# A decode block whose scheduler context is closed behind the first loads

## The chip, the cores and the metric

The kernel runs on one core of a Trainium2 chip. The metric is the device time of one execution in microseconds (us). A time stands for the median of several executions; a profile is one further execution, recorded instruction by instruction, and its span runs from the first to the last recorded instruction.

## What is computed

The reference is one decode step of a block with four sequences (B = 4), one new token each, and D = 512 channels. All numbers are 32-bit floats.

```python
xn = _layernorm(x, axis=-1)
return x + _A_ref(xn, A_k_cache, A_v_cache, A_wq, A_wo) + _B_ref(xn, B_w1, B_w2, B_w3, B_w4)
```

`_A_ref` is attention over a cache: 32 heads of 128 channels, 4096 cached keys and values per sequence and head. With `q = xn @ wq`:

```python
scores = jnp.einsum("bhqd,bhkd->bhqk", q, k_cache) * (Dh ** -0.5)
p = _softmax(scores, axis=-1)
o = jnp.einsum("bhqk,bhkd->bhqd", p, v_cache)
```

and `o`, with its heads side by side, is multiplied by `wo`. `_B_ref` has a token mixing that shifts along the sequence; with one token every shifted part is zero, so `x1 = xn`, and what is left of it is `x1 + _gelu(_layernorm(x1) @ w3) @ w4`, with F = 1792 hidden channels. The two caches are 268 MB each and make up nearly all the data.

## The kernel before, in words

The caches are cut into 32 blocks of four heads (NJ = 32, LAST = 31). One block of K or of V is 128 partitions by 16,384 elements, 8 MB. There is room for three such blocks: `ks[0]` and `ks[1]`, which K uses in turn, and `vs`, which V uses. The weights borrow the same room: at the start w3 and several small tiles (`ident`, `wide`, `xs`, `lnc`) lie in `vs` and wq in `ks[1]`; at the end w4 comes into `vs`, the last V block into `ks[0]` and wo into `ks[1]`.

The order of the work is written out by hand. The whole program, but for its last wait, stands in one critical section (line 168) of a scheduling context: the scheduler doesn't reorder what is inside, and the kernel's own class `Steps` (lines 53 to 83) sets the semaphores. `do(engine, make, *after)` makes the engine wait for the listed steps, issues the instruction and lets it increment that engine's own semaphore (nPE, nDVE, nACT, nPOOL). `load` (line 165) does the same for a transfer, by default from SP's queue.

Setup (lines 175 to 264): SP issues the loads of w3, wq and K block 0 (k0), ACT the load of x. POOL makes `ident` and clears some tiles, DVE writes two constants, and then one chain runs: layer norm of x on DVE with its square root on ACT (L198 to L205), transpose on PE (L211), second layer norm, second transpose, the product with w3 (L234), GELU on DVE and ACT (L238 to L247), the query product with wq (L255), scaling and transposes of q (L259 to L262).

The loads of the caches (lines 271 to 284) all stand in SP's queue, each behind a wait: K block 1 waits for the query product (it takes wq's place), V block 0 for GELU and q, each later K block for `summed` (DVE has reduced the block that was there) and each later V block for `done` (the block before has been used and copied). At the end SP issues w4 and five pieces of wo.

Three loops run side by side, one on each engine. DVE (L300) multiplies a K block by q (L320) and sums over channels (L321) in two halves, then takes the maximum of the rows. ACT (L334) makes the exponentials (L339) and copies results out of PSUM. PE (L384) multiplies the exponentials by the V block (L373) and selects and sums (L378, L380). The last V block stands behind the loop.

The ending: products with w4 (L396) and wo (L410, and L152 by quarter columns into `total`), a copy to SBUF (L421), and four stores of 2 KB, two on SP's queue and two on ACT's (L423), each of which adds 16 to the semaphore `out`. Then the critical section ends; a second one (line 427) holds one wait of SP for `out` to be 64. Where the context is left, the framework adds what the profile puts on lines 168, 427 and 452: drains, by which each engine reports that it has finished its instructions, semaphores and branches between the sections, then a barrier of all five engines, a clear of the semaphores by POOL, and a second barrier.

Of the kernel before, what the change touches and what calls it, by code (L numbers as in the profile page):

```python
# [44 lines left out]
P = 128  # L45
# [7 lines left out]
class Steps:  # L53
# [33 lines left out]
def decode_block(ctx: ExitStack, tc: tile.TileContext, x, k, v, wq, wo, w3, w4, out):  # L87
# [61 lines left out]
    def blocks4(start, stop, w, m, src):  # L149
# [18 lines left out]
    with tc.tile_critical():  # L168
# [11 lines left out]

        ident0 = do("POOL", lambda e: e.memset(ident, 0.0))

        ident_ok = do("POOL", lambda e: e.affine_select(
            out=ident, in_=ident, compare_op=ALU.not_equal, fill=1.0, base=0, pattern=[[-1, P]],
            channel_multiplier=1), ident0)
        xnT = X.rearrange("p c b -> p (c b)").rearrange("p (c m) -> p c m", c=NC)
        x1nT = lts[:, 0].rearrange("p h q -> p (h q)").rearrange("p (c m) -> p c m", c=NC)
        xnT0 = do("POOL", lambda e: e.memset(xnT, 0.0))
        x1nT0 = do("POOL", lambda e: e.memset(x1nT, 0.0))
        rs0 = do("POOL", lambda e: e.memset(rs, 0.0))  # L190
        ones_ok = do("DVE", lambda e: e.memset(ones, 1.0))
        eps_ok = do("DVE", lambda e: e.memset(eps, EPS))


        lnq = os.rearrange("p m d -> p (m d)")[:B, :]

        def layernorm(src, o, s, *after):
            d = do("DVE", lambda e: e.reduce_sum(s[:, 0:1], src, axis=AX.X), *after)  # L198
            d = do("DVE", lambda e: e.tensor_scalar_mul(s[:, 0:1], s[:, 0:1], 1.0 / D), d)
            d = do("DVE", lambda e: e.tensor_scalar(lnc, src, s[:, 0:1], None, op0=ALU.subtract), d)  # L200
            d = do("DVE", lambda e: e.tensor_mul(lnq, lnc, lnc), d)
            d = do("DVE", lambda e: e.reduce_sum(s[:, 1:2], lnq, axis=AX.X), d)
            a = do("ACT", lambda e: e.activation(s[:, 2:3], s[:, 1:2], AF.Sqrt, bias=eps[:B], scale=1.0 / D), d, eps_ok)
            d = do("DVE", lambda e: e.reciprocal(s[:, 3:4], s[:, 2:3]), a)
            return do("DVE", lambda e: e.tensor_scalar_mul(o, lnc, s[:, 3:4]), d)  # L205

        def transposed(src, o, p, *after):

            do.wait("PE", after)
            for c in range(NC):  # L210
                i = lambda e: e.matmul(p[:, c, :], src.rearrange("b (p c) -> b c p", c=NC)[:, c, :], ident[:B, :B],  # L211
                                       start=True, stop=True)
                d = do("PE", i)
            return do("DVE", lambda e: e.tensor_copy(o[:, :, 0:B], p), d, xnT0, x1nT0)

        pw_row = pw.rearrange("p g m -> p (g m)")
        xn, x1n = pw_row[:B, 0:D], pw_row[:B, D:2 * D]
        ptn = pt.rearrange("p (n c b) -> p n c b", n=32, c=NC)
        xn_ok = layernorm(xs, xn, lns[:B, 0], x_in)
        sel_ok = do("DVE", lambda e: e.reduce_sum(sel, ident.rearrange("p (q m) -> p m q", q=G), axis=AX.X), ident_ok)  # L220
        mask_ok = do("DVE", lambda e: e.reduce_sum(mask, ident.rearrange("p (q m) -> p q m", q=G), axis=AX.X))
        xnT_ok = transposed(xn, xnT, ptn[:, 0], xn_ok, ident_ok)
        x1n_ok = layernorm(xn, x1n, lns[:B, 1], xn_ok)

        do.wait("PE", [x_in])
        blocks4(True, False, ident[:B, 0:32], 32, xs)
        total_ok = do("PE", lambda e: blocks4(False, False, ident[:B, 0:32], 32, xn))
        x1nT_ok = transposed(x1n, x1nT, ptn[:, 1], x1n_ok, xnT_ok)


        do.wait("PE", [x1nT_ok, w3_in])
        for c in range(NC):
            for t in range(4):
                up = lambda e: e.matmul(y[32 * t:32 * t + 32, :FT], x1nT[:, c, :], w3_sb[:, c, t * FT:(t + 1) * FT],  # L234
                                        start=(c == 0), stop=(c == NC - 1))
                d = do("PE", up)
        hs, u, th, gt = (vs[:, n * FT:(n + 1) * FT] for n in range(4))
        a = do("ACT", lambda e: e.copy(hs.rearrange("p (m i) -> p m i", i=32),  # L238
                                       y[:, :FT].rearrange("p (i m) -> p m i", i=32)), d)
        d = do("DVE", lambda e: e.tensor_mul(u, hs, hs), a)  # L240
        d = do("DVE", lambda e: e.tensor_scalar(u, u, GELU_B, 1.0, op0=ALU.mult, op1=ALU.add), d)
        d = do("DVE", lambda e: e.tensor_mul(u, u, hs), d)
        a = do("ACT", lambda e: e.activation(th, u, AF.Tanh, scale=GELU_A), d)
        d = do("DVE", lambda e: e.tensor_scalar(th, th, 1.0, 0.5, op0=ALU.add, op1=ALU.mult), a)
        d = do("DVE", lambda e: e.tensor_mul(hs, hs, th), d)
        d = do("DVE", lambda e: e.transpose(gt, hs), d)
        gT_ok = do("DVE", lambda e: e.tensor_copy(gT, gt.rearrange("p (m i) -> p m i", i=32)[:, :, 0:B]), d)  # L247


        wq_h = wq_sb.rearrange("p c (n j h d) -> p c n h j d", n=2, j=4, h=G)  # L250
        do.wait("PE", [xnT_ok, wq_in])
        for c in range(NC):
            for n in range(2):
                for h in range(G):
                    q = lambda e: e.matmul(pq[n][HP * h:HP * h + HP, :], xnT[:, c, :], wq_h[:, c, n, h],  # L255
                                           start=(c == 0), stop=(c == NC - 1))
                    pq_ok = do("PE", q)
        for n in range(2):
            a = do("ACT", lambda e: e.mul(pw_row[:, n * 4 * DH:(n + 1) * 4 * DH], pq[n], DH ** -0.5), pq_ok)  # L259
        d = do("DVE", lambda e: e.transpose(wide, pw_row), a)  # L260
        pw_ok = do("POOL", lambda e: e.memset(pw, 0.0), d)
        qT_ok = do("DVE", lambda e: e.tensor_copy(  # L262
            qT.rearrange("p (b i) n -> p b i n", b=B),
            wide.rearrange("p (i n m) -> p m i n", n=DH // HP, m=32)[:, 0:B]), d)
# [3 lines left out]
        SUMMED = [(sems["summed"], 2 * j + 2) for j in range(NJ)]  # L268
        DONE = [(sems["done"], j + 1) for j in range(NJ)]
        HALF = R * DH // 2  # L270
        load(ks[1], rows(kf, 1), "k1", None, pq_ok)
        load(vs, rows(vf, 0), "landed", None, gT_ok, qT_ok, total_ok)
        parts = [load(ks[0][:, n:n + HALF], rows(kf, 2)[:, n:n + HALF], f"half{i}", 16, (sems["summed"], i + 1))
                 for i, n in enumerate((0, HALF))]
        for j in range(LAST - 1):
            if j > 0:
                load(ks[j % 2], rows(kf, j + 2), f"k{j % 2}", None, SUMMED[j])
            load(vs, rows(vf, j + 1), "landed", None, DONE[j])
        last_in = load(ks[(LAST - 1) % 2], rows(vf, LAST), "last", 16, SUMMED[LAST - 1])
        w4_in = load(w4_sb, w4.rearrange("(p m) n -> p m n", m=NF), "w4", 16, DONE[LAST - 1])  # L280
        do.wait("SP", [SUMMED[LAST]])
        wo_r = wo.rearrange("(p c) n -> p c n", c=WC)
        for (c0, c1), sem in zip(wo_cuts, wo_sems):
            nc.sync.dma_start(wo_sb[:, c0:c1], wo_r[:, c0:c1]).then_inc(sem, 16)  # L284
        def take(engine, sem, n=1):

            engine.wait_ge(sems[sem], n)
            engine.sem_inc(sems[sem], -n)  # L288
# [11 lines left out]
        with nc.Fori(0, NJ // 2, engines=OrderedEngineSet([DVE]), head_slot={DVE: 128}) as j:  # L300
            e, n = nc.vector, 0

            def step(i, done="dve"):
                nonlocal n
                if n:
                    i.wait_op(sems["dve"], n, "sem-ge")
# [150 lines left out]
```

## Time and profile before

| | |
|---|---|
| time before, median of 3 runs | 1305.08 us (1304.96 to 1305.3) |
| span of the profiled execution | 1303.1 us |
| TensorE clock granted, mean over the span | 0.629 |
| DVE busy | 1164.2 us, 89% |
| PE busy | 366.4 us, 28% |
| ACT busy | 93.1 us, 7% |
| read from HBM | 561.00 MB |

The profiled execution has no separate time of its own beside its span. In the profile's rows, PE is TensorE, DVE is VectorE, ACT is ScalarE, POOL is GpSimd and SP is SyncE; a q behind the name (SPq) stands for the engine's sequencer, which issues transfers and handles semaphores and is not counted as busy. A row of the timeline gives the start, the length, the engine, the source line, the operation, what is written and read, and in brackets how long the engine was idle before and what ended that. A row by source line gives a count, the least, the median and the greatest duration in nanoseconds, and the start of the first and the last instruction. Tiles stand without their buffer number, so `ks` is either of `ks[0]` and `ks[1]`.

### The profile page before, as it was taken

How to read it: one execution, taken by the hardware profiler on the slowest of the kernel's cores; microseconds unless marked ns; L12 is line 12 of the kernel's file. 1: busy time of each engine (PE TensorE's matmuls, PEld its weight loads, DVE VectorE, ACT ScalarE, POOL GpSimd, SP SyncE). 2: the span in 40 equal slices, each digit the busy share in tenths (PEclk: the TensorE clock that was granted, in tenths of full speed). 3: DMA queues.
4: the chain of work that ended last, by engine and by line, in shares of the span. 5: the costliest groups of instructions: out<-in, count | busy, mean ns of one | idle time of the engine just before them, and what ended most of it. 6: DMA issues, size and time to landing. Idle time of an engine off the chain costs nothing. (4 is left out here: it accounts for less than half of the span.)

```text
span 1303.1 us, 6697 instructions
## 1 busy us (share of the span) xinstructions
PE 366.4 (28%) x2652; PEld 131.4 (10%) x2652; DVE 1164.2 (89%) x324; ACT 93.1 (7%) x330; POOL 2.4 (0%) x12
## 2 busy tenths in 40 slices
PE   3221233321233331133332123332122332113237
PEld 1000111100011110011110011110001111001112
DVE  3499999999999999999999999999999999999990
ACT  1000000000000000000000000000000000000000
POOL 0000000000000000000000000000000000000000
PEclk8655666655666665666665666665566666566668
DMA  9999999999999999999999999999999999999998
GB/s 403 444 422 445 428 439 430 435 430 437 430 428 441 424 445 424 445 424 441 428 439 430 437 430 435 433 428 439 424 445 424 445 424 443 426 439 430 437 422 350
DMA packets 10559, 561.10 MB, mean 431 GB/s; under 512 B 1188, under 2 KB 1204, under 8 KB 1464
## 3 DMA queue, kind: packets, MB, share of 16 engines
q1 hardware_dynamic: 10528, 561.00, 99.6%
q8 instruction: 4, 0.07, 0.0%
q14 instruction: 3, 0.02, 0.0%
q10 hardware_dynamic: 24, 0.01, 0.0%
HBM read 561.00 MB, written 0.01 MB: 431 GB/s over the span
## 5 line engine op out<-in xcount | busy, mean ns | idle before, releaser
L320 DVE TENSOR_TENSOR ks<-ks,qb 128x8192 f32<-128x8192 f32 x64 | 556.3, 8692 | 60.4 <-DVEq L288 55.4
L321 DVE TENSOR_REDUCE sc<-ks 128x64 f32<-128x8192 f32 x64 | 555.9, 8686 | 2.2
L373 PE MATMUL pv<-vs,pw 128*32 128x512 f32 x1984 | 284.3, 737 | 872.8 <-PEq L288 872.8
L373 PEld LDWEIGHTS pv<-vs,pw 128*32 128x32 f32 x1984 | 78.0, 132 | 1054.6 <-issue 1054.6
L344 ACT COPY os<-pv 128x512 f32<-128x512 f32 x32 | 18.8, 586 | 825.1 <-ACTq L288 825.1
L339 ACT ACTIVATE pw<-sc,small 32x128 f32<-32x128 f32 x128 | 51.0, 398 | 278.0 <-ACTq L288 276.8
L378 PE MATMUL poz<-sel,os 128*128 128x4 f32 x256 | 32.8, 252 | 28.2 <-PEq L288 28.2
L378 PEld LDWEIGHTS poz<-sel,os 128*128 128x128 f32 x256 | 31.0, 191 | 56.3 <-issue 56.3
L339 ACT ACTIVATION_READ_ACCUMULATOR pw<-sc,small 32x1 f32 x128 | 23.5, 184 | 0.0
L260 DVE STREAM_TRANSPOSE vs<-pw 128x1024 f32<-128x1024 f32 x1 | 1.2, 1245 | 17.2 <-ACT pw L259 17.2
L421 DVE COPY sc<-total 128x128 f32<-128x128 f32 x1 | 0.3, 290 | 16.4 <-PE total L152 16.4
L326 DVE TENSOR_REDUCE small<-sc 128x1 f32<-128x128 f32 x32 | 9.2, 286 | 4.7
L354 DVE RECIPROCAL rz<-oz 128x96 f32<-128x96 f32 (+1 forms) x2 | 1.1, 552 | 12.4 <-ACT oz L346 12.3
L380 PE MATMUL poz<-rs,ones 128*128 128x4 f32 x64 | 11.7, 253 | 0.0
L312 DVE STREAM_TRANSPOSE qb<-qg 128x128 f32<-128x128 f32 x32 | 10.0, 311 | 1.1
L311 DVE COPY qg<-qT 128x4 f32 x32 | 5.4, 170 | 5.5 <-issue 4.7
L380 PEld LDWEIGHTS poz<-rs,ones 128*128 128x128 f32 x64 | 9.7, 192 | 0.0
L346 ACT COPY oz<-poz 128x8 f32 x32 | 5.3, 166 | 50.9 <-ACTq L288 50.9
L410 PE MATMUL y<-ks,X 128*4 128x512 f32 x48 | 7.8, 818 | 3.5 <-DMA ks<-in_A_wo_dram 3.5
L255 PE MATMUL pv<-ks,X 128*32 128x512 f32 x32 | 5.0, 709 | 12.3 <-DMA ks<-in_A_wq_dram 12.3
L373 PE MATMUL pv<-ks,pw 128*32 128x512 f32 x64 | 8.3, 674 | 0.0
L327 DVE STREAM_TRANSPOSE tr<-small 128x32 f32<-128x32 f32 x32 | 6.8, 212 | 1.1
(72 smaller groups left out, 67.1 us busy)
## 6 DMA issues: line engine op xcount, KB each, us to landing
ks<-in_A_k_cache_dram SPq DMA_DIRECT2D x2, 4096.0 KB, 26.9
vs<-in_B_w_dram SPq DMA_DIRECT2D x2, 3584.0 KB, 13.6
ks<-in_A_wo_dram SPq DMA_DIRECT2D x1, 4096.0 KB, 21.7
ks<-in_A_wo_dram SPq DMA_DIRECT2D x1, 2048.0 KB, 26.3
ks<-in_A_wo_dram SPq DMA_DIRECT2D x1, 1024.0 KB, 28.3
ks<-in_A_wo_dram SPq DMA_DIRECT2D x1, 768.0 KB, 29.7
ks<-in_A_k_cache_dram SPq DMA_DIRECT2D x31, 42.2
vs<-in_A_v_cache_dram SPq DMA_DIRECT2D x31, 26.9
```

Of the source, the lines that this page charges most:

```text
L311: step(e.tensor_copy(qg, pairs[:, s, bass.ds(j, 1)].rearrange("p o n -> p (o n)")))
L312: step(e.transpose(qb.rearrange("p (n m) -> p n m", m=HP), qg.unsqueeze(2).to_broadcast([P, DH // HP, HP])))
L320: step(e.tensor_tensor(out=kt, in0=kt, in1=qb.unsqueeze(1).to_broadcast([P, w, DH]), op=ALU.mult))
L321: step(e.reduce_sum(sc[s][:, c:c + w], kt, axis=AX.X))
L326: step(e.reduce_max(rm, sc[s], axis=AX.X))
L327: step(e.transpose(tr[s], rm.to_broadcast([P, HP])))
L339: i = nc.scalar.activation(pw[hp, :, 4 * h:4 * h + 4], sc[s][hp, :].rearrange("p (g w) -> p g w", w=4), AF.Exp, bias=small[hp, s, 1:2], sc ...
L344: nc.scalar.copy(os, pv.rearrange("p (m d) -> p m d", m=4)).then_inc(sems["copied"], 1)
L373: i = nc.tensor.matmul(pv[32 * t:32 * t + 32, :], pw[:, g, :], vt[:, 4 * g:4 * g + 4, :], start=(g < 4), stop=(g >= NG - 4))
L378: nc.tensor.matmul(poz[:, 0:G], os[:, m, :], sel.rearrange("p (h m) -> p m h", m=4)[:, m, 0:G], start=(m == 0), stop=(m == 3))
L380: nc.tensor.matmul(poz[:, G:2 * G], ones.to_broadcast([P, P]), rs, start=True, stop=True).then_inc(sems["poz"], 1)
L410: i = nc.tensor.matmul(y[32 * t:32 * t + B, :], X[:, c, :], wo_sb[:, c], start=False, stop=(c >= 20))
```

## The change

Semaphores and tiles come straight from the core's program (`nc`) and not from the scheduling context (`tc`) and its pools. The critical section holds the first four loads alone; behind it the context is closed, which issues its drains, its two barriers and its semaphore clear at that place. All that follows has the same instructions in the same order, now one indentation further left and outside the context. At the end SP and ACT increment a new semaphore `bye` once their stores are issued; POOL waits for 2 and clears all the kernel's semaphores but `out`; SP waits for `out` and takes 64 off it.

```diff
-    def __init__(self, tc):
-        self.tc, nc = tc, tc.nc
+    def __init__(self, nc):
...
-        self.sem = {e: tc.alloc_semaphore(f"n{e}") for e in ("PE", "DVE", "ACT", "POOL")}
+        self.sem = {e: nc.alloc_semaphore(f"n{e}") for e in ("PE", "DVE", "ACT", "POOL")}
...
-    consts = ctx.enter_context(tc.tile_pool(name="consts", bufs=1))
-    psum = ctx.enter_context(tc.tile_pool(name="psum", bufs=1, space=PSUM))
-
     def sb(name, *shape):
-        return consts.tile([P, *shape], F32, name=name)
+        return nc.alloc_sbuf_tensor(name, [P, *shape], F32).ap()
 
     def bank(name):
-        return psum.tile([P, 4 * DH], F32, name=name)
+        return nc.alloc_psum_tensor(name, [P, 4 * DH], F32).ap()
...
-    do = Steps(tc)
-    sems = {n: tc.alloc_semaphore(n) for n in (
-        "x", "w3", "wq", "k0", "k1", "landed", "last", "w4", "go", "pv", "copied", "poz", "out",
-        "half0", "half1", "nm", "dve", "summed", "expd", "done")}
-    wo_sems = [tc.alloc_semaphore(f"wo{n}") for n in range(5)]
+    do = Steps(nc)
+    wo_sems = [nc.alloc_semaphore(f"wo{n}") for n in range(5)]
+    sems = {n: nc.alloc_semaphore(n) for n in (
+        "x", "w3", "wq", "k0", "k1", "landed", "last", "w4", "go", "pv", "copied", "poz",
+        "half0", "half1", "nm", "dve", "summed", "expd", "done", "bye", "out")}
...
         k_in = {0: load(ks[0], rows(kf, 0), "k0", 16)}
 
+    tc.close()
+    tc.compile()
+
...
-    with tc.tile_critical():
-        do.wait("SP", [stored])
+    nc.sync.sem_inc(sems["bye"], 1)
+    nc.scalar.sem_inc(sems["bye"], 1)
+    nc.gpsimd.wait_ge(sems["bye"], 2)
+    nc.clear_and_free_semaphores([*do.sem.values(), *wo_sems, *(h for n, h in sems.items() if n != "out")])
+    do.wait("SP", [stored])
+    nc.sync.sem_inc(sems["out"], -64)
```

More of the change, by code (lines that the diff above doesn't have):

```diff
@@ L178, in decode_block @@
         k_in = {0: load(ks[0], rows(kf, 0), "k0", 16)}
[L181 to L231, printed above, removed]
-        for c in range(NC):
[L233 to L257, printed above, removed]
@@ L258, in decode_block @@
-        for n in range(2):
[L259 to L288, printed above, removed]
@@ L383, in decode_block @@
-        do.wait("PE", [sel_ok, mask_ok, ones_ok, a])
-        with nc.Fori(0, LAST, engines=OrderedEngineSet([PE]), head_slot={PE: 0}):
-            values(lambda: take(nc.tensor, "landed", 16), vs)
-        xb = pt.rearrange("p (b c) -> p b c", b=B * 4)
-        for b in range(B - 1):
-            d = do("PE", lambda e: e.matmul(xb[:, b, :], lts[:, b].rearrange("p h q -> p (h q)"), sel, start=True, stop=True),
-                   LTS[b])
-        values(lambda: do.wait("PE", [last_in]), ks[(LAST - 1) % 2])
@@ L393, in decode_block @@
-        do.wait("PE", [w4_in, g4_ok])
-        for m in range(NF):
-            t, g, n = (m, g4[:, m, :], 32) if m < 4 else (m % 4, gT[:, m, :], B)
-            nc.tensor.matmul(y[32 * t:32 * t + n, :], g, w4_sb[:, m, :], start=(m < 4), stop=False)
-        d = do("PE", lambda e: e.matmul(xb[:, B - 1, :], lts[:, B - 1].rearrange("p h q -> p (h q)"), sel, start=True,
-                                        stop=True), LTS[B - 1])
-        X_ok = do("ACT", lambda e: e.copy(X.rearrange("p c b -> p b c"), xb[:, 0:B, :]), d)
@@ L420, in decode_block @@
-        r = sc[0]
-        d = do("DVE", lambda e: e.tensor_copy(r, total), d)
-        for t in range(4):
-            stored = do("SP" if t % 2 == 0 else "ACT", lambda e: e.dma_start(
-                out.rearrange("b s d -> (b s) d")[:, P * t:P * t + P], r[32 * t:32 * t + B, :]), d,
-                done=(sems["out"], 16, 64))
-    with tc.tile_critical():
-        do.wait("SP", [stored])
+    tc.close()
+    tc.compile()
+    ident0 = do("POOL", lambda e: e.memset(ident, 0.0))
+    ident_ok = do("POOL", lambda e: e.affine_select(
+        out=ident, in_=ident, compare_op=ALU.not_equal, fill=1.0, base=0, pattern=[[-1, P]],
+        channel_multiplier=1), ident0)
@@ new lines, in transposed @@
+    def transposed(src, o, p, *after):
+        do.wait("PE", after)
+        for c in range(NC):
+            i = lambda e: e.matmul(p[:, c, :], src.rearrange("b (p c) -> b c p", c=NC)[:, c, :], ident[:B, :B],
+                                   start=True, stop=True)
+            d = do("PE", i)
+        return do("DVE", lambda e: e.tensor_copy(o[:, :, 0:B], p), d, xnT0, x1nT0)
+    pw_row = pw.rearrange("p g m -> p (g m)")
+    xn, x1n = pw_row[:B, 0:D], pw_row[:B, D:2 * D]
+    ptn = pt.rearrange("p (n c b) -> p n c b", n=32, c=NC)
@@ new lines, in decode_block @@
+    xn_ok = layernorm(xs, xn, lns[:B, 0], x_in)
+    sel_ok = do("DVE", lambda e: e.reduce_sum(sel, ident.rearrange("p (q m) -> p m q", q=G), axis=AX.X), ident_ok)
+    mask_ok = do("DVE", lambda e: e.reduce_sum(mask, ident.rearrange("p (q m) -> p q m", q=G), axis=AX.X))
+    xnT_ok = transposed(xn, xnT, ptn[:, 0], xn_ok, ident_ok)
+    x1n_ok = layernorm(xn, x1n, lns[:B, 1], xn_ok)
+    do.wait("PE", [x_in])
+    blocks4(True, False, ident[:B, 0:32], 32, xs)
+    total_ok = do("PE", lambda e: blocks4(False, False, ident[:B, 0:32], 32, xn))
@@ new lines, in decode_block @@
+    x1nT_ok = transposed(x1n, x1nT, ptn[:, 1], x1n_ok, xnT_ok)
+    do.wait("PE", [x1nT_ok, w3_in])
+    for c in range(NC):
+        for t in range(4):
+            up = lambda e: e.matmul(y[32 * t:32 * t + 32, :FT], x1nT[:, c, :], w3_sb[:, c, t * FT:(t + 1) * FT],
+                                    start=(c == 0), stop=(c == NC - 1))
+            d = do("PE", up)
+    hs, u, th, gt = (vs[:, n * FT:(n + 1) * FT] for n in range(4))
+    a = do("ACT", lambda e: e.copy(hs.rearrange("p (m i) -> p m i", i=32),
+                                   y[:, :FT].rearrange("p (i m) -> p m i", i=32)), d)
@@ new lines, in decode_block @@
+    wq_h = wq_sb.rearrange("p c (n j h d) -> p c n h j d", n=2, j=4, h=G)
+    do.wait("PE", [xnT_ok, wq_in])
+    for c in range(NC):
+        for n in range(2):
+            for h in range(G):
+                q = lambda e: e.matmul(pq[n][HP * h:HP * h + HP, :], xnT[:, c, :], wq_h[:, c, n, h],
+                                       start=(c == 0), stop=(c == NC - 1))
+                pq_ok = do("PE", q)
+    for n in range(2):
+        a = do("ACT", lambda e: e.mul(pw_row[:, n * 4 * DH:(n + 1) * 4 * DH], pq[n], DH ** -0.5), pq_ok)
@@ new lines, in decode_block @@
+    d = do("DVE", lambda e: e.transpose(wide, pw_row), a)
+    pw_ok = do("POOL", lambda e: e.memset(pw, 0.0), d)
+    qT_ok = do("DVE", lambda e: e.tensor_copy(
+        qT.rearrange("p (b i) n -> p b i n", b=B),
+        wide.rearrange("p (i n m) -> p m i n", n=DH // HP, m=32)[:, 0:B]), d)
+    SUMMED = [(sems["summed"], 2 * j + 2) for j in range(NJ)]
+    DONE = [(sems["done"], j + 1) for j in range(NJ)]
+    HALF = R * DH // 2
+    load(ks[1], rows(kf, 1), "k1", None, pq_ok)
+    load(vs, rows(vf, 0), "landed", None, gT_ok, qT_ok, total_ok)
@@ new lines, in decode_block @@
+    parts = [load(ks[0][:, n:n + HALF], rows(kf, 2)[:, n:n + HALF], f"half{i}", 16, (sems["summed"], i + 1))
+             for i, n in enumerate((0, HALF))]
+    for j in range(LAST - 1):
+        if j > 0:
+            load(ks[j % 2], rows(kf, j + 2), f"k{j % 2}", None, SUMMED[j])
+        load(vs, rows(vf, j + 1), "landed", None, DONE[j])
+    last_in = load(ks[(LAST - 1) % 2], rows(vf, LAST), "last", 16, SUMMED[LAST - 1])
+    w4_in = load(w4_sb, w4.rearrange("(p m) n -> p m n", m=NF), "w4", 16, DONE[LAST - 1])
@@ new lines, in decode_block, with take @@
+    do.wait("SP", [SUMMED[LAST]])
+    wo_r = wo.rearrange("(p c) n -> p c n", c=WC)
+    for (c0, c1), sem in zip(wo_cuts, wo_sems):
+        nc.sync.dma_start(wo_sb[:, c0:c1], wo_r[:, c0:c1]).then_inc(sem, 16)
+    def take(engine, sem, n=1):
+        engine.wait_ge(sems[sem], n)
+        engine.sem_inc(sems[sem], -n)
+    nc.gpsimd.sem_inc(sems["expd"], 2)
+    do.wait("POOL", parts)
+    nc.gpsimd.sem_inc(sems["k0"], 16)
+    d = do("POOL", lambda e: e.memset(g4, 0.0), DONE[LAST - 1])
+    g4_ok = do("POOL", lambda e: e.tensor_copy(g4[:, :, 0:B], gT[:, 0:4, :]), d, gT_ok)
@@ new lines, in decode_block, with step @@
+    do.wait("DVE", [qT_ok])
+    pairs = qT.rearrange("p (j s) n -> p s j n", s=2)
+    with nc.Fori(0, NJ // 2, engines=OrderedEngineSet([DVE]), head_slot={DVE: 128}) as j:
+        e, n = nc.vector, 0
+        def step(i, done="dve"):
+            nonlocal n
+            if n:
+                i.wait_op(sems["dve"], n, "sem-ge")
+            i.then_inc(sems[done], 1)
+            n += done == "dve"
+        for s in range(2):
+            step(e.tensor_copy(qg, pairs[:, s, bass.ds(j, 1)].rearrange("p o n -> p (o n)")))
+            step(e.transpose(qb.rearrange("p (n m) -> p n m", m=HP), qg.unsqueeze(2).to_broadcast([P, DH // HP, HP])))
+            take(e, "expd")
+            take(e, f"k{s}", 16)
+            w = R // 2
+            for c in range(0, R, w):
+                kt = ks[s].rearrange("p (c d) -> p c d", c=R)[:, c:c + w]
+                step(e.tensor_tensor(out=kt, in0=kt, in1=qb.unsqueeze(1).to_broadcast([P, w, DH]), op=ALU.mult))
+                step(e.reduce_sum(sc[s][:, c:c + w], kt, axis=AX.X))
+                e.wait_ge(sems["dve"], n)
+                e.sem_inc(sems["summed"], 1)
+            rm, nm = small[:, s, 0:1], small[:, s, 1:2]
+            step(e.reduce_max(rm, sc[s], axis=AX.X))
+            step(e.transpose(tr[s], rm.to_broadcast([P, HP])))
+            step(e.tensor_reduce(nm, tr[s], axis=AX.X, op=ALU.max, negate=True), "nm")
+        take(e, "dve", n)
@@ new lines, in decode_block @@
+    do.wait("ACT", [pw_ok, rs0])
+    ozs = oz.rearrange("p n (j s h) -> p s n j h", s=2, h=G)
+    with nc.Fori(0, NJ // 2, engines=OrderedEngineSet([ACT]), head_slot={ACT: 128}) as j:
+        for s in range(2):
+            take(nc.scalar, "nm")
+            for h in range(G):
+                hp = slice(HP * h, HP * h + HP)
+                i = nc.scalar.activation(
+                    pw[hp, :, 4 * h:4 * h + 4], sc[s][hp, :].rearrange("p (g w) -> p g w", w=4), AF.Exp,
+                    bias=small[hp, s, 1:2], scale=1.0, accum_out=rs[hp, h:h + 1])
+            i.then_inc(sems["go"], 1)
+            take(nc.scalar, "pv")
+            nc.scalar.copy(os, pv.rearrange("p (m d) -> p m d", m=4)).then_inc(sems["copied"], 1)
+            take(nc.scalar, "poz")
+            nc.scalar.copy(ozs[:, s, :, bass.ds(j, 1)].rearrange("p n o h -> p n (o h)"),
+                           poz[:, 0:2 * G].rearrange("p (n h) -> p n h", n=2)).then_inc(sems["done"], 1)
@@ new lines, in decode_block, with spread @@
+    LTS = {}
+    def spread(b0, b1):
+        s = slice(H * b0, H * b1)
+        d = do("DVE", lambda e: e.reciprocal(rz[:, s], oz[:, 1, s]), DONE[ZB * b1 - 1])
+        d = do("DVE", lambda e: e.tensor_mul(ot[:, s], oz[:, 0, s], rz[:, s]), d)
+        n = H * (b1 - b0)
+        d = do("DVE", lambda e: e.tensor_mul(lts.rearrange("p b h q -> p (b h) q")[:, s],
+                                             ot[:, s].unsqueeze(2).to_broadcast([P, n, 4]),
+                                             mask.unsqueeze(1).to_broadcast([P, n, 4])), d)
+        LTS.update(dict.fromkeys(range(b0, b1), d))
@@ new lines, in decode_block, with values @@
+    spread(0, B - 1)
+    spread(B - 1, B)
+    def values(landed, rows_of):
+        take(nc.tensor, "go")
+        nc.tensor.sem_inc(sems["expd"], 1)
+        landed()
+        vt = rows_of.rearrange("p (c d) -> p c d", c=R)
+        for g in range(NG):
+            t = g % 4
+            i = nc.tensor.matmul(pv[32 * t:32 * t + 32, :], pw[:, g, :], vt[:, 4 * g:4 * g + 4, :],
+                                 start=(g < 4), stop=(g >= NG - 4))
+        i.then_inc(sems["pv"], 1)
+        take(nc.tensor, "copied")
+        for m in range(4):
+            nc.tensor.matmul(poz[:, 0:G], os[:, m, :], sel.rearrange("p (h m) -> p m h", m=4)[:, m, 0:G],
+                             start=(m == 0), stop=(m == 3))
+        nc.tensor.matmul(poz[:, G:2 * G], ones.to_broadcast([P, P]), rs, start=True,
+                         stop=True).then_inc(sems["poz"], 1)
@@ new lines, in decode_block @@
+    do.wait("PE", [sel_ok, mask_ok, ones_ok, a])
+    with nc.Fori(0, LAST, engines=OrderedEngineSet([PE]), head_slot={PE: 0}):
+        values(lambda: take(nc.tensor, "landed", 16), vs)
+    xb = pt.rearrange("p (b c) -> p b c", b=B * 4)
+    for b in range(B - 1):
+        d = do("PE", lambda e: e.matmul(xb[:, b, :], lts[:, b].rearrange("p h q -> p (h q)"), sel, start=True, stop=True),
+               LTS[b])
+    values(lambda: do.wait("PE", [last_in]), ks[(LAST - 1) % 2])
+    do.wait("PE", [w4_in, g4_ok])
@@ new lines, in decode_block @@
+    for m in range(NF):
+        t, g, n = (m, g4[:, m, :], 32) if m < 4 else (m % 4, gT[:, m, :], B)
+        nc.tensor.matmul(y[32 * t:32 * t + n, :], g, w4_sb[:, m, :], start=(m < 4), stop=False)
+    d = do("PE", lambda e: e.matmul(xb[:, B - 1, :], lts[:, B - 1].rearrange("p h q -> p (h q)"), sel, start=True,
+                                    stop=True), LTS[B - 1])
+    X_ok = do("ACT", lambda e: e.copy(X.rearrange("p c b -> p b c"), xb[:, 0:B, :]), d)
+    ys = os.rearrange("p m d -> p (m d)")
@@ new lines, in decode_block @@
+    do.wait("PE", [X_ok])
+    for (c0, c1), sem in zip(wo_cuts, wo_sems):
+        do.wait("PE", [(sem, 16)])
+        for c in range(c0, c1):
+            if c < 24:
+                t = (c + 2) % 4
+                i = nc.tensor.matmul(y[32 * t:32 * t + B, :], X[:, c, :], wo_sb[:, c], start=False, stop=(c >= 20))
+            else:
+                i = blocks4(False, c == WC - 1, X[:, c, :], B, wo_sb[:, c])
+        d = do("PE", lambda e: i)
+        if c1 == 24:
+            ys_ok = do("ACT", lambda e: e.copy(ys, y), d)
+        elif c1 == 28:
+            do.wait("PE", [ys_ok])
+            blocks4(False, False, sel, 32, ys)
@@ new lines, in decode_block @@
+    r = sc[0]
+    d = do("DVE", lambda e: e.tensor_copy(r, total), d)
+    for t in range(4):
+        stored = do("SP" if t % 2 == 0 else "ACT", lambda e: e.dma_start(
+            out.rearrange("b s d -> (b s) d")[:, P * t:P * t + P], r[32 * t:32 * t + B, :]), d,
+            done=(sems["out"], 16, 64))
+    nc.sync.sem_inc(sems["bye"], 1)
+    nc.scalar.sem_inc(sems["bye"], 1)
+    nc.gpsimd.wait_ge(sems["bye"], 2)
+    nc.clear_and_free_semaphores([*do.sem.values(), *wo_sems, *(h for n, h in sems.items() if n != "out")])
```

117 lines of the change are left out of this document (25 added, 92 removed).

## The prediction

> **What bounds the kernel now.** I read the page first: engine shares, queues, the slices.
>
> ```profile
> span 1303.1 us, 6697 instructions
> ...
> PE 366.4 (28%) x2652; PEld 131.4 (10%) x2652; DVE 1164.2 (89%) x324; ACT 93.1 (7%) x330; POOL 2.4 (0%) x12
> ...
> DMA  9999999999999999999999999999999999999998
> ...
> q1 hardware_dynamic: 10528, 561.00, 99.6%
> ```
>
> Queue q1 (SP's loads, 561 MB) keeps the 16 DMA engines busy for 99.6% of the span. DVE with 89% comes close but has room. The view by windows, cut at the four places where the stages change, shows where the other 0.4% lie (length of the stretch, busy time of the engines, then PEclk, DMA share, GB/s):
>
> ```profile
> 0.00:1.00 1.00, 0.00 (x0) 0.00 (x0) 0.00 (x0) 0.00 (x0) 0.26 (x5) 1.00 0.00 0
> ...
> 2.40:45.00 42.60, 18.49 (x128) 7.79 (x128) 13.27 (x29) 4.47 (x8) 0.95 (x1) 0.88 0.98 424
> 45.00:1298.50 1253.50, 346.86 (x2492) 122.89 (x2492) 1150.52 (x293) 87.71 (x322) 0.40 (x2) 0.62 1.00 433
> 1298.50:1303.10 4.60, 1.06 (x32) 0.67 (x32) 0.29 (x1) 0.00 (x0) 0.00 (x0) 0.80 0.02 5
> ```
>
> So time can be won or lost at three places only: the first microsecond, in which nothing is loaded; the last 4.6 us, in which nothing is loaded any more; and any moment between at which the queue would run dry. The chain that ended last says what those 4.6 us are (start, length, what):
>
> ```profile
> 1268.85 29.66 DMA ks<-in_A_wo_dram
> 1298.52 0.04 issue
> 1298.56 1.10 PE total L152 x32
> 1299.66 0.02 issue
> 1299.68 0.29 DVE sc L421
> ```
>
> The last piece of wo lands at 1298.5, PE and DVE finish at 1299.97. The remaining 3.2 us are stores and closing, which the chain leaves out; the view by source line has them (count, ns, start of the first and the last):
>
> ```profile
> L423 SPq DMA_DIRECT2D out_dram<-sc x2: 280/316/352, 1300.0 to 1300.4; - x2
> L423 ACTq DMA_DIRECT2D out_dram<-sc x2: 278/292/307, 1300.0 to 1300.3; - x2
> ...
> L168 SPq EVENT_SEMAPHORE  x3: 17/28/28, 1301.1 to 1301.4; - x3
> ...
> L168 SPq DRAIN  x1: 18/18/18, 1301.2 to 1301.2; - x1
> L168 SPq NOP  x1: 18/18/18, 1301.4 to 1301.4; - x1
> ...
> L452 SPq EVENT_SEMAPHORE  x1: 98/98/98, 1301.7 to 1301.7; - x1
> L452 SPq COMPARE_BRANCH  x1: 38/38/38, 1301.9 to 1301.9; - x1
> ...
> L427 SPq NOP  x1: 13/13/13, 1302.2 to 1302.2; - x1
> ...
> L452 SPq DRAIN  x2: 7/7/7, 1302.2 to 1302.3; - x2
> ...
> L452 POOLq DRAIN  x1: 106/106/106, 1302.5 to 1302.5; - x1
> ...
> L452 POOLq EVENT_SEMAPHORE_RANGE_CLEAR  x1: 225/225/225, 1302.6 to 1302.6; - x1
> ...
> L452 POOLq EVENT_SEMAPHORE  x1: 17/17/17, 1303.0 to 1303.0; - x1
> L452 SPq EVENT_SEMAPHORE  x1: 17/17/17, 1303.1 to 1303.1; - x1
> L452 PEldq EVENT_SEMAPHORE  x1: 51/51/51, 1303.1 to 1303.1; - x1
> ```
>
> The stores are issued from 1300.0 to 1300.7 (1300.4 + 0.3). The EVENT_SEMAPHORE of 98 ns at 1301.7 stands last before the branch; it is SP's wait for all four stores, and it ends at 1301.8. From there to the end, 1303.1 − 1301.8 = 1.3 us, only bookkeeping runs: a branch, SP's own drain and NOP, two barriers of all engines, and between them POOL's range clear of 225 ns.
>
> **The change, part by part.** *The end.* In the changed order of instructions SP issues its stores, adds one to bye, waits for out, and is done with that; nothing follows on any engine. What follows the wait in the rows above (1.3 us) is removed. The only new work is POOL's: wait for bye, drain, one range clear. SP's first instruction behind its stores stands at 1301.1 in the rows, so bye is complete by then at the latest; its drain and clear took from 1302.5 to 1302.8 in the old closing (1302.6 + 0.225), 0.3 us and at most 0.4; POOL is done by 1301.5, 0.3 us ahead of the end of the store wait. It sits beside the stores' flight and costs nothing. If that cover were gone (bye later than 1301.4), each later 0.1 us would cost 0.1 us. The gain at the end is 1.3 us; at least 0.9 (the two barriers alone, 1302.2 to 1303.1), at most 1.3 inside the span.
>
> That the wait ends at 1301.8 rests on the trace: the last store's issue starts at 1300.4, so issue to landing is 1.4 us. The Trainium skill, DMA: Bandwidth & Descriptors, section "Anatomy of one DMA — SWDGE (gpsimd) path", gives about 2.0 us fixed for one transfer, on another issuing path. By it the stores would land at 1302.4, an estimate from that page, and 0.7 us would be left to win (1304.4 us). The measured 1.4 us decides.
>
> *The beginning.* The closing block moves behind the four loads. Its rows:
>
> ```profile
> 0.94 0.20 POOL L181 MEMSET vs<- 128x128 f32 x1 [0.50 <-SPq L168]
> ...
> 1.02 0.06 DVE L191 MEMSET ones<- 128x1 f32 x1 [1.02 <-SPq L168]
> ...
> 1.38 0.29 POOL L183 TENSOR_SCALAR_AFFINE_SELECT vs<-vs 128x128 f32<-128x128 f32 x1 [0.23 <-POOL vs L181]
> ...
> 1.52 1.28 ACT L203 ACT_TABLE_LOAD   x1 [1.52 <-SPq L168]
> ...
> 1.89 0.42 SPq L166 DMA_DIRECT2D ks<-in_A_k_cache_dram  x1
> ...
> 2.51 0.67 DVE L198 TENSOR_REDUCE lns<-vs 4x1 f32<-4x512 f32 x1 [1.41 <-DMA vs<-in_A_x_dram]
> ...
> 5.33 0.29 ACT L203 ACTIVATE lns<-lns,eps 4x1 f32<-4x1 f32 x1 [2.53 <-DVE lns L202]
> ...
> 6.37 2.02 PE L211 MATMUL pt<-vs,pw 4*128 4x4 f32 x8 [6.37 <-DVE pw L205]
> ...
> 14.66 4.79 PE L234 MATMUL y<-vs,lts 128*32 128x448 f32 x32 [0.27 <-DVE lts L214]
> ...
> 31.72 1.08 PE L255 MATMUL pv<-ks,X 128*32 128x512 f32 x4 [12.27 <-DMA ks<-in_A_wq_dram]
> ...
> 40.52 0.33 SPq L166 DMA_DIRECT2D ks<-in_A_k_cache_dram  x1
> ...
> 51.99 8.69 DVE L320 TENSOR_TENSOR ks<-ks,qb 128x8192 f32<-128x8192 f32 x1 [6.72 <-DVEq L288]
> ```
>
> Nothing stands ahead of the first load that wasn't there, so the transfers begin as before. SP issues its third load until 1.89 + 0.42 = 2.31 and only then reaches the barriers. Priced by the old end, where the same kind of instructions ran: issue end to the NOP of L168, 1300.7 to 1301.4, 0.7; a branch, 0.2 (1301.9 to the next block); two barriers with the clear, 0.9. That opens the second barrier at 2.3 + 1.8 = 4.1 us. Least is 3.2 (barriers alone); most is 4.7 (the whole stretch from 1300.7 to 1303.1, store wait included, 2.4). DVE's two memsets (0.1 us) then precede L198, which starts at 4.2 instead of 2.51: 1.7 late, 0.8 to 2.3 between the bounds. ACT's table load then ends at 4.1 + 1.28 = 5.4, ahead of the square root that needs it (5.33 + 1.7 = 7.0). POOL starts 3.2 late, so ident is there at 1.67 + 3.2 = 4.9, ahead of the first transpose on PE, which waits for the norm anyway (6.37 + 1.7 = 8.1).
>
> Queued behind the delay is one chain: two norms, two transposes, the w3 product on PE, then the query product. PE stands idle 12.27 us before that product because wq hasn't landed. So 1.7 us late turns into 10.5 us of idle time in place of 12.27, the query product still starts at 31.72, and SP's next load (ks, 40.52) leaves on time. Cost zero, covered by the flight of wq. Without that cover it would be 1.7 us on k1's issue, and even that the queue absorbs: k0 is in flight until 52.0 (DVE's L320 waits for it), 11.5 us behind the issue at 40.52.
>
> *All else.* Tiles from pools become plain allocations, at the same places in SBUF and PSUM; loops, waits and every compute instruction stay. Cost zero; a bound can't be read from any row, since nothing changes that a row measures.
>
> **Sum.** The profiled execution: span 1303.1 us − 1.3 + 0 = 1301.8. The median of the runs is 1305.08, 1.98 above that span; kept, that gives 1305.08 − 1.3 = 1303.8 us, or 0.10% less.
>
> **The rivals.** *(1) The end gains more than its own 1.3 us.* PE and DVE are free at 1300.0 instead of 1303.1. If part of the 1.98 us outside the span is each engine's own closing, that part now overlaps the stores. For: the rows show all engines held in the two barriers until 1303.1. Against: SP, which the time then hangs on, still has its own share. With all of it saved 1301.8, with half 1302.8; as a rival with two thirds, 1302.5.
> The Trainium skill, Runtime: NRT & Kernel Launch, section "The launch sequence", speaks against this one: a barrier of all engines and a semaphore reset follow the kernel, so early engines would only wait there. No row here shows that stretch.
>
> *(2) No gain, 1305.1.* The engines have to meet somewhere; without the barriers the 1.3 us come back outside the span. For: 1.98 us outside are unexplained. Against: those two microseconds already stand behind barriers that met twice, and a fixed closing doesn't grow.
>
> *(3) Slower: the drain behind the loads waits for their data.* SP's DRAIN now stands behind three large loads (w3, wq, k0). If it held until k0 landed, the barrier would open at 52.0 + 0.9 = 52.9. From L198 to the end of the w3 product it takes 14.66 + 4.79 − 2.51 = 16.9 us, the query product 40.52 − 31.72 = 8.8: k1 would be issued at 78.6, and the DMA engines would stand idle for 26.6 us from 52.0. 1305.08 + 26.6 − 1.3 = 1330.4. It decides only from a point on: the delay must pass 12.3 (PE's idle time) + 11.5 (queue left) = 23.8 us before any DMA time is lost. Against: at the old end the SP DRAIN of L168 stood behind two stores, ran at 1301.2 for 18 ns, and the wait for those stores ended at 1301.8 only. A drain that waits for transfers would have ended there.
>
> *(4) The change doesn't do what it says.* The closing block could be emitted again at the end. The changed order of instructions has no barrier there; I put this with (2).
>
> **How the numbers follow.** Forecast 1303.8: 74%; its own range 1303.3 to 1304.5: on one side a quarter of what lies outside (0.5) on top, on the other the least gain of 0.9 (1304.2) and the 0.3 by which the three runs differ. Rival (1) 13%, as it needs a saving that no row shows; (2) with (4) 9%; (3) 4%, as one row contradicts it. The range 1302.2 to 1305.4 holds the forecast, (2) and most of (1), and leaves (3) out. A measurement of this kernel tells about 0.2% (2.6 us) from no change, so faster means under 1302.5: the lower part of (1), 11% in all; slower, over 1307.7: (3) and 1% unnamed, 5%; the same: 84%.
>
> **What would show it.** Right: a span near 1301.8; the last instruction SP's wait for out, ending 1.8 us behind the issue of the first store; POOL's range clear before it; two barriers and a clear between 2.3 and 5 us; L198's counterpart near 4.2; PE's idle time before the query product near 10.5; k1 issued near 40.5; q1 still at 99.6% or above. Wrong: a layer norm that starts behind 26 us, a DMA slice below 9 near the beginning, POOL's clear as the last instruction, or a span shorter by 1.3 with an unchanged time.

## The result and the profile after

The changed kernel takes 1303.33 us (median of 21 runs, 1303.17 to 1303.51) against 1305.08 us before (21 runs, 1304.89 to 1305.36): 1.75 us less, a ratio of 0.9986 with a 95% interval of 0.998 to 0.9992. The two ranges of the runs don't touch. The forecast was 1303.8 us, 1.3 less.

Each run, the profiled one too, has both a time and a span. Over the runs (21 of the changed kernel, 27 of the one before), the mean span went from 1303.29 to 1301.96 us (1.3 less, the forecast of the sum), and what lies outside it, time minus span, from 1.80 to 1.37 us. These further 0.43 us were in the prediction as a rival only. The page of the profile after:

```profile
span 1301.9 us, 6687 instructions
...
PE 367.0 (28%) x2652; PEld 132.2 (10%) x2652; DVE 1164.2 (89%) x324; ACT 93.0 (7%) x330; POOL 2.4 (0%) x12
...
q1 hardware_dynamic: 10528, 561.00, 99.7%
```

The loads still bound the kernel, with the same bytes. The end, by source line, in the changed kernel:

```profile
L422 SPq DMA_DIRECT2D out_dram<-sc x2: 273/310/347, 1300.1 to 1300.5; - x2
L422 ACTq DMA_DIRECT2D out_dram<-sc x2: 277/294/310, 1300.1 to 1300.4; - x2
...
L427 ACTq EVENT_SEMAPHORE  x1: 17/17/17, 1300.7 to 1300.7; - x1
...
L426 SPq EVENT_SEMAPHORE  x1: 17/17/17, 1300.8 to 1300.8; - x1
...
L429 POOLq DRAIN  x1: 99/99/99, 1300.8 to 1300.8; - x1
L429 POOLq EVENT_SEMAPHORE_RANGE_CLEAR  x1: 196/196/196, 1300.9 to 1300.9; - x1
...
L431 SPq EVENT_SEMAPHORE  x1: 17/17/17, 1301.9 to 1301.9; - x1
```

The issue of the last store begins at 1300.5 and SP's wait for all four ends the span at 1301.9, 1.4 us later, as before the change; the branch, the two barriers and the clear that stood behind it are gone. POOL is done at 1301.1, inside the stores' flight. The beginning, first by source line, then from the timeline:

```profile
L164 SPq DRAIN  x1: 55/55/55, 2.4 to 2.4; - x1
...
L177 SPq DRAIN  x3: 7/7/7, 2.7 to 3.0; - x3
...
L177 POOLq EVENT_SEMAPHORE_RANGE_CLEAR  x1: 51/51/51, 3.0 to 3.0; - x1
...
L177 SPq EVENT_SEMAPHORE  x2: 17/17/17, 2.9 to 3.3; - x2
```

```profile
3.48 0.67 DVE L197 TENSOR_REDUCE lns<-vs 4x1 f32<-4x512 f32 x1
...
31.84 1.94 PE L254 MATMUL pv<-ks,X 128*32 128x512 f32 x8 [11.55 <-DMA ks<-in_A_wq_dram]
...
40.93 0.33 SPq L162 DMA_DIRECT2D ks<-in_A_k_cache_dram  x1
...
52.03 8.69 DVE L319 TENSOR_TENSOR ks<-ks,qb 128x8192 f32<-128x8192 f32 x1 [6.33 <-DVEq L287]
```

SP's drain behind the loads takes 55 ns at 2.4 us, with all three large loads in flight, and the second barrier opens at 3.3. The first norm starts at 3.48 instead of 2.51, PE is idle 11.55 us before the query product instead of 12.27, and the first multiplication with K starts at 52.03 instead of 51.99. Most of the delay ended in the wait for wq, as forecast; K block 1 is issued 0.4 us later than before (40.93 against 40.52), which the start of that multiplication doesn't show.

### The profile page after: what moved, and what is told of

The parts are those of the page before. It is cut to its first block, busy times and chain, and to the rows that moved or that the text cites. A ratio compares the mean times of both kernels' runs of the same rounds, so it can differ in the third digit from the quotient of the medians.

```text
span 1301.9 us, 6687 instructions
## 1 busy us (share of the span) xinstructions
PE 367.0 (28%) x2652; PEld 132.2 (10%) x2652; DVE 1164.2 (89%) x324; ACT 93.0 (7%) x330; POOL 2.4 (0%) x12
```

## The experiments

All are the changed kernel with one edit. Where engines are held below, a new semaphore `end` makes them wait for SP at the very end (`take` waits for a semaphore and takes off what it waited for); POOL's clear leaves `end` out. The kernel before was measured beside each of them, with medians of 1305.00 to 1305.09 us; so times of kernels that weren't measured side by side compare to about 0.1 us only.

**1. Where the 0.43 us outside the span come from.** First, all four other engines are held until SP has waited for the stores:

```diff
     do.wait("SP", [stored])
     nc.sync.sem_inc(sems["out"], -64)
+    nc.sync.sem_inc(sems["end"], 4)
+    take(nc.tensor, "end")
+    take(nc.vector, "end")
+    take(nc.scalar, "end")
+    take(nc.gpsimd, "end")
```

> PE, DVE, ACT and POOL are held at the end until SP has waited for the stores; the closing block of before is not brought back. The span should end 0.1 us later than that of the changed kernel (1302.0 against 1301.9: one increment by SP, one wait and one decrement on each engine). Theory A (the 0.5 us that the change won outside the span come from engines that are done early): they are lost again, 1303.3 + 0.1 + 0.5 = 1303.9 us, and time minus span goes back from 1.4 to 1.9. Theory B (they come from the missing closing block itself, whenever the engines are done): 1303.4 us, time minus span stays at 1.4.

Measured: 1304.02 us (11 runs), mean span 1302.20, time minus span 1.89. The loss is back although the old closing block is not; theory A holds and B falls. Then POOL's drain and clear were moved behind the store wait:

```diff
-    nc.sync.sem_inc(sems["bye"], 1)
     nc.scalar.sem_inc(sems["bye"], 1)
-    nc.gpsimd.wait_ge(sems["bye"], 2)
-    nc.clear_and_free_semaphores([...])
     do.wait("SP", [stored])
     nc.sync.sem_inc(sems["out"], -64)
+    nc.sync.sem_inc(sems["bye"], 1)
+    nc.gpsimd.wait_ge(sems["bye"], 2)
+    nc.clear_and_free_semaphores([...])
```

> POOL's drain and range clear are put behind SP's wait for the stores, the cover of the stores' flight is taken away from them. Both theories: the span grows by what stands uncovered, drain 0.1 + clear 0.2 + two semaphore steps 0.1 = 0.4 us, to 1302.3. Theory A: POOL is late as well now, so the time grows by 0.4 us and by up to a further 0.5 if it is POOL's own closing that counts: 1303.7 to 1304.2 us. Theory B: 1303.7 us. If the clear had been free for another reason than its cover: 1303.3.

Measured: 1304.31 us (11 runs), 0.98 more. In the profiled execution the clear is the last thing in the span of 1302.4 us; by source line:

```profile
L428 SPq EVENT_SEMAPHORE  x1: 17/17/17, 1302.0 to 1302.0; - x1
...
L431 POOLq DRAIN  x1: 99/99/99, 1302.1 to 1302.1; - x1
L431 POOLq EVENT_SEMAPHORE_RANGE_CLEAR  x1: 196/196/196, 1302.2 to 1302.2; - x1
```

The span grew by 0.47 (mean 1302.43), the price of the uncovered clear; the other half, time minus span of 1.86 instead of 1.37, comes with POOL being last. So theory A was sharpened. Theory P: outside the span each engine has a closing of its own length, and the time is the latest of (engine's end + its closing). Its rival Q: the engines have to meet, so any engine held to the end costs the same. POOL alone, then PE alone was held, with the edit of the first run cut to one engine and an increment of 1:

> Only POOL is held until SP has waited for the stores; its range clear stays early. Theory P (each engine has a closing of its own outside the span, and POOL's is the longest): span 1302.0 to 1302.1, time minus span 1.9, so 1303.9 to 1304.0 us, as with all four engines held. Theory C (it was the late range clear, or another engine): 1303.4 to 1303.5 us, time minus span 1.4.

> Only PE is held. Theory P: PE's closing isn't longer than SP's, span 1302.1, time minus span 1.4, 1303.5 us. Theory Q (any engine that ends last beside SP costs the 0.5, because the engines have to meet): 1304.0 us.

POOL alone: 1303.99 us (11 runs), as much as all four together, with its clear as early as ever. By source line, the last instructions of that kernel and of the one that holds PE:

```profile
L431 SPq EVENT_SEMAPHORE  x1: 17/17/17, 1301.9 to 1301.9; - x1
...
L287 POOLq EVENT_SEMAPHORE  x1: 17/17/17, 1302.0 to 1302.0; - x1
```

```profile
L287 PEldq EVENT_SEMAPHORE  x1: 51/51/51, 1302.0 to 1302.0; - x1
```

In both the last instruction stands at 1302.0, yet the one with PE last takes 1303.73 us (11 runs), 0.26 less. Q falls: it matters which engine is last. P's guess that PE's closing is no longer than SP's was a miss; it lies between. Two more runs let another engine than SP wait for the stores:

```diff
-    do.wait("SP", [stored])
-    nc.sync.sem_inc(sems["out"], -64)
+    do.wait("DVE", [stored])
+    nc.vector.sem_inc(sems["out"], -64)
```

> DVE waits for the stores and takes 64 off out, SP ends at its bye (1300.8). Theory P: the time is the latest of the engines' ends plus each one's own closing; SP now ends early, POOL at 1301.1 + 1.9 = 1303.0, DVE at 1301.9 plus a closing that no run has shown. 1303.0 us if that is 1.1 or less, 1303.3 if it is as long as SP's 1.4. Theory Q: the engines meet, so 1303.3 us whoever waits.

> The same with ACT as the one that waits. Theory P: between 1303.0 us (ACT's closing 1.1 or less) and 1303.8 (1.9, as long as POOL's). Theory Q: 1303.3 us.

Measured: 1303.52 us with DVE, 1303.46 us with ACT (same edit with ACT), 11 runs each. Neither gains on SP. All runs by the engine that ends last (times are medians, spans and differences means over the runs):

| kernel | ends last | time | span | time − span |
|---|---|---|---|---|
| changed | SP | 1303.33 | 1301.96 | 1.37 |
| DVE waits for the stores | DVE | 1303.52 | 1302.09 | 1.47 |
| ACT waits for the stores | ACT | 1303.46 | 1301.96 | 1.51 |
| PE held | PE | 1303.73 | 1302.05 | 1.67 |
| before | all, at the barrier | 1305.09 | 1303.29 | 1.80 |
| POOL's clear last | POOL | 1304.31 | 1302.43 | 1.86 |
| all four held | four | 1304.02 | 1302.20 | 1.89 |
| POOL held | POOL | 1303.99 | 1302.09 | 1.90 |

(Before: 27 runs, beside those with all four held and with the clear last.) The five kernels further below, which also end with SP, have 1.36 to 1.40 in the last column. The kernel before fits as well: there POOL's last instruction stands 0.1 us ahead of the last one of all, and 1.90 − 0.1 = 1.80. What the engines do in that time no record shows, nor whether they meet there on ways of different length; that the time from the last instruction to the end depends on the engine, and that POOL's is the longest, is what the runs show.

**2. Whether the loads' flight is the cover at the beginning.** The context is closed ahead of the loads:

```diff
-    with tc.tile_critical():
+    tc.close()
+    tc.compile()
...
     k_in = {0: load(ks[0], rows(kf, 0), "k0", 16)}
-    tc.close()
-    tc.compile()
```

> The context is closed ahead of the four loads instead of behind them, so the two barriers and the clear stand in front of the first transfer. In the changed kernel they took 2.67 to 3.31 us, 0.64 us. If the loads' flight is what covers them there, the first load is issued at about 1.5 instead of 0.96 and the whole stream of loads shifts: 1303.3 + 0.55 = 1303.9 us. If the first microsecond didn't matter (the queue catches up later), 1303.3 us.

Measured: 1303.85 us (11 runs), 0.52 more. The timeline of SP in that kernel, and its last instruction by source line:

```profile
1.39 0.40 SPq L162 DMA_DIRECT2D vs<-in_B_w_dram  x1
```

```profile
L429 SPq EVENT_SEMAPHORE  x1: 17/17/17, 1302.4 to 1302.4; - x1
```

The first load leaves at 1.39 instead of 0.96, and the end comes 0.5 us later. The barriers that cost nothing behind the loads cost 0.5 us ahead of them. That is a little less than the 0.64 us that they take; the edit also removes the critical section, whose entry stood ahead of the loads.

**3. How much delay the setup can take.** The first norm was made to wait for a load as well, for w3, wq or k0:

```diff
+    do.wait("DVE", [w3_in])
     xn_ok = layernorm(xs, xn, lns[:B, 0], x_in)
```

> The first layer norm also waits for w3, so the setup's chain starts at 14.4 us instead of 3.5, 11 late, just within PE's 11.6 us of idle time ahead of the query product. Cover theory: the w3 product ends at 31.5, the query product starts where it did (31.8), 1303.3 us. If late microseconds counted: up to 1314.

> The first layer norm also waits for wq, so the chain of the setup starts at 31.8 us instead of 3.5, 28.3 late. In the changed kernel it takes 17.1 us from the norm to the end of the w3 product, so the query product starts at 48.9 instead of 31.8 and k1 is issued at 58.0 instead of 40.9. Cover theory: k0 has landed at 52.0, the queue is dry for 6 us and up to 2 more until the first bytes of k1: 1309.3 to 1311.3 us. If every late microsecond counted: 1303.3 + 28.3 = 1331.6. If the stream made up for it later: 1303.3.

> The first layer norm waits for k0, the price of the rival in which the drain behind the loads holds until they have landed. From the run with wq: the chain from the norm (31.7) to the query product (48.9) takes 17.2 us and the product about 7, so with the norm at 52.0 k1 is issued at 76 to 78; the queue is dry from 52 on, 24 to 26 us and about 2 more until data flow again: 1327 to 1332 us, against 1330.4 in the prediction.

With w3: 1303.34 us (11 runs), no loss. The timeline of that kernel:

```profile
12.05 0.67 DVE L197 TENSOR_REDUCE lns<-vs 4x1 f32<-4x512 f32 x1 [8.51 <-DMA vs<-in_B_w_dram]
...
31.41 1.07 PE L255 MATMUL pv<-ks,X 128*32 128x512 f32 x8 [1.39 <-DMA ks<-in_A_wq_dram]
...
38.62 0.33 SPq L162 DMA_DIRECT2D ks<-in_A_k_cache_dram  x1
```

w3 had landed by 12.05 us and not, as expected, at 14.4. A norm 8.6 us later than in the changed kernel vanishes in PE's idle time, of which 1.39 us are left. The kernel before took 1305.00 us beside this one, so a loss of up to 0.1 us could hide. With wq: 1311.40 us (4 runs), 8.1 more and just above the expected range. Its timeline:

```profile
31.66 0.67 DVE L197 TENSOR_REDUCE lns<-vs 4x1 f32<-4x512 f32 x1 [27.88 <-DMA ks<-in_A_wq_dram]
...
48.91 1.03 PE L255 MATMUL pv<-ks,X 128*32 128x512 f32 x8
...
56.10 0.33 SPq L162 DMA_DIRECT2D ks<-in_A_k_cache_dram  x1
```

The norm is 28.2 us late, k1's issue 56.10 − 40.93 = 15.2, the end 8.1: of the delay of k1, 7.1 us are free. With k0: 1330.83 us (2 runs, 1330.25 and 1331.4), 27.5 more. Timeline, then the view by windows of that kernel (the last two numbers are DMA share and GB/s):

```profile
50.75 0.67 DVE L197 TENSOR_REDUCE lns<-vs 4x1 f32<-4x512 f32 x1 [47.20 <-DMA ks<-in_A_k_cache_dram]
...
76.09 0.33 SPq L162 DMA_DIRECT2D ks<-in_A_k_cache_dram  x1
```

```profile
48.00:50.00 2.00, 0.00 (x0) 0.00 (x0) 0.00 (x0) 0.00 (x0) 0.00 (x0) 1.00 0.00 0
50.00:76.00 26.00, 18.10 (x128) 7.86 (x128) 10.77 (x25) 2.98 (x5) 0.00 (x0) 1.00 0.00 1
76.00:79.00 3.00, 0.00 (x0) 0.00 (x0) 1.75 (x2) 1.08 (x2) 0.49 (x1) 1.00 1.01 350
```

A dry queue looks like this: next to nothing begins to move from 48 on, and only what was begun before is finished, until k1 is issued at 76.1. k0 has landed at 50.75 here, where nothing competes with it, and not at 52.0.

**4. An attempt at a version faster than both.** By theory P the time hangs on SP's end. DVE and ACT each copy two of the four result blocks side by side, and each queue issues one store of 4 KB in place of two of 2 KB:

```diff
-    r = sc[0]
-    d = do("DVE", lambda e: e.tensor_copy(r, total), d)
-    for t in range(4):
...
+    for n, (e, q) in enumerate((("DVE", "SP"), ("ACT", "ACT"))):
+        for t in (2 * n, 2 * n + 1):
+            cut = ys[0:B, P * t:P * t + P], total[32 * t:32 * t + B, :]
+            c = do(e, lambda g: g.tensor_copy(*cut) if e == "DVE" else g.copy(*cut), d)
+        stored = do(q, lambda g: g.dma_start(out.rearrange("b s d -> (b s) d")[:, 2 * P * n:2 * P * n + 2 * P],
+                                             ys[0:B, 2 * P * n:2 * P * n + 2 * P]), c, done=(sems["out"], 16, 32))
...
-    nc.sync.sem_inc(sems["out"], -64)
+    nc.sync.sem_inc(sems["out"], -32)
```

> DVE and ACT each copy two of the four blocks side by side into four partitions, and each queue issues one store of 4 KB instead of two of 2 KB. Theory P (the time is the latest of the engines' ends plus each one's own closing: SP 1.4, POOL 1.9): in the changed kernel the first store of a queue is written to memory by 1301.0 and the second by 1301.35, so SP's wait ends 0.35 us earlier, less up to 0.1 for the second copy; SP 1301.5 + 1.4 = 1302.9, POOL done at 1300.8 + 1.9 = 1302.7. 1302.9 to 1303.1 us, span 1301.5 to 1301.7. If the landing takes its 1.4 us whatever the number of stores: 1303.3.

Measured: 1303.17 us (11 runs, 1303.05 to 1303.37), ratio to before 0.9986 (0.9977 to 0.9995), mean span 1301.79. By source line:

```profile
L422 DVE COPY os<-total x2: 279/280/281, 1299.9 to 1300.2; 4x128 f32<-4x128 f32 x2
...
L423 SPq DMA_DIRECT2D out_dram<-os x1: 348/348/348, 1300.5 to 1300.5; - x1
...
L431 SPq EVENT_SEMAPHORE  x1: 17/17/17, 1301.9 to 1301.9; - x1
```

The 0.35 us that SP's end should have gained didn't come. A copy of 4 × 128 takes 280 ns, hardly less than the 290 of the whole 128 × 128, so the two in a row let SP's only store leave at 1300.5, when the changed kernel issues its second one. The landing takes 1.4 us from the last issue either way. The medians differ by 0.16 us, with ranges that overlap, and the kernel before was 0.08 us faster beside this one than beside the changed one; the ratio to before is the same 0.9986. That is too little to call it faster than the changed kernel. It is faster than the kernel before, by as much as the changed one.

## Why the prediction was right, point by point

**The end, −1.3 inside the span: right.** Mean span 1303.29 to 1301.96. The wait that ends at 1301.8 in the old rows became the last instruction, 1.4 us behind the last store's issue. The 2.0 us of the Trainium skill (DMA: Bandwidth & Descriptors, "Anatomy of one DMA — SWDGE (gpsimd) path"), stated there for another issuing path, would have left 0.7; the traces before and after both have 1.4 for these stores.

**POOL's clear costs nothing: right in the span, but the margin was read at the wrong place.** It ends at 1301.1, 0.8 us before SP, better than the 0.3 of the prediction, since bye is complete at 1300.8 already. But POOL's closing is 0.5 us longer than SP's (1.90 against 1.37), so by theory P what counts is 1301.1 + 1.9 = 1303.0 against 1301.9 + 1.4 = 1303.3: 0.3 us of cover, not 0.8. No run delays the clear by so little, so these 0.3 us are worked out and not measured. Uncovered, the clear costs 0.98 and not its own 0.4.

**Time minus span kept as it was: the step that failed.** The prediction carried 1.98 us (median minus the span of the one profiled execution; the mean over the runs is 1.80) over unchanged. It fell by 0.43. The time stays inside the forecast's own range (1303.3 to 1304.5) by 0.03 us, and only because its lower end allowed 0.5 us outside the span, for which the sum had no mechanism; that much is luck. Rival (1) named the effect, but as a sum to be saved by all engines' early end; the runs show it is one engine's, POOL's, whose place at the end SP took. The Trainium skill's rule that was set against the rival (Runtime: NRT & Kernel Launch, "The launch sequence": behind the kernel a barrier of all engines and a reset follow) doesn't foresee it: by that rule, as the prediction drew on it, early engines only wait, and holding POOL would have cost the 0.1 us by which the span grew. It cost 0.66. Rival (2), no gain, falls with the 1.75 us.

**The beginning: the cost of zero is right, its price was too high.** The second barrier opened at 3.3, not 4.1: behind the issue of the third load it took 1.0 us instead of 1.8 (SP's steps up to its drain at 2.7 took 0.4 instead of 0.9, the two barriers with the clear 0.6 instead of 0.9). It lies just above the least of 3.2 that was given. The norm came 1.0 us late instead of 1.7.

**Rival (3): rightly dismissed, and rightly priced for a wrong reason.** The drain took 55 ns. The run that waits for k0 came to 1330.83 us, against 1330.4. Yet the point from which it decides was wrong: not 12.3 + 11.5 = 23.8 us of delay, but about 20. Behind wq the norm is 28.2 us late and the end 8.1, so 20.1 us are free: 11.1 in PE's wait for wq, 1.9 because the query product then takes less time, and 7.1 in the queue. Behind k0 it is 47.3 − 27.5 = 19.8. The 11.5 took DVE's start at 52.0 for the moment at which the queue runs dry. k0 alone lands at 50.75, and the free 7.1 us end at 48.0, 2.7 us ahead of that: the next transfer has to be issued before the one ahead of it has landed. About 0.9 us of the 2.7 is its own start (k1, issued at 76.1 in that run, begins to move at 77.0); the rest is open. That the price came out at 1330 is luck: the norm starts at 50.75 and not at 52.9, as that run has no barriers behind the landing; 27.5 us are lost and not 26.6; and they count from 1303.3 and not from 1303.8.

## What to carry to other kernels

A closing barrier is worth as much as it is exposed: behind the last store it cost 1.3 us, ahead of the first load 0.5, behind the loads nothing. When only microseconds are left at the end, look at which engine ends last as well as when: here 0.5 us lay between SP and POOL. And measure slack by making the thing late: the start of a consumer says when its data had landed with everything else in flight, not when the queue runs dry.

## What had not been expected of the hardware

Time minus span depends on the engine that ends last: 1.37 us for SP, 1.47 for DVE, 1.51 for ACT, 1.67 for PE, 1.86 to 1.90 for POOL. And PE's query product was faster behind a late norm: with the norm behind w3 it follows the w3 product after 1.39 us and k1 is issued 38.62 − 31.41 = 7.2 us after its start, against 40.93 − 31.84 = 9.1 behind an idle time of 11.55 us; the first eight matmuls take 1.07 us instead of 1.94. The profile's rows show the granted clock beside it: from 31 to 35 us it is 0.50 in the changed kernel and 1.00 in the one with w3, the same factor of about two as the matmuls. Why the clock is lower there was not tried. The time shows nothing of it, as the queue doesn't run dry there in either kernel.
